# Four 128x32 matmuls in place of one 128x128 while attention runs, and w_in loaded in column quarters

## The chip, the cores and the metric

The kernel runs on one core of one Trainium2 chip. The metric is the device time of one execution in microseconds, as the median of several runs. Before the change it was 392.27 us (three runs, 391.82 to 393.17).

A core has one instruction stream for each engine: TensorE (PE, with its weight loads listed as PEld), VectorE (DVE), ScalarE (ACT), GpSimd (POOL) and SyncE (SP). [...] Loads here are issued by POOL, stores by SP and ACT.

## The reference

```python
scores = matmul(q, k.T) / sqrt(64)          # q, k, v: 8 batches x 12 heads x 448 tokens x 64
attn   = softmax(scores) @ v
x      = attn as 3584 tokens x 768
h      = x @ w_in                           # w_in: 768 x 2048
out    = (h * sigmoid(h)) @ w_out           # w_out: 2048 x 768, out: 3584 x 768 float32
```

The kernel takes and gives float32 in memory. Its loads convert to float16, and its sums are float32 in PSUM.

## The kernel before

**Attention.** Each batch has three groups of four heads. A unit is one batch, one group and a range of query tokens (batch 0 is cut in two pieces of 224 tokens, the other batches have one piece of 448). For a unit, `scores` (L376) multiplies K by Q with 32-row matmuls, four of them side by side because each head uses 32 rows of the array. `expo` (L412) takes the exponential on ACT. `attend` (L438) multiplies the exponentials by V, and `attend_sums` (L453) sums them; both use 128x32 matmuls, four side by side, one for each head and so for each 32 columns of the array. VectorE turns K and Q (L359, L369), inverts the sums and scales the result into x (L545).

**MoE.** `ffn1` (L557) multiplies x by w_in: six 128x128 matmuls for each 128 columns of w_in. ACT and VectorE make the activation (L573, L598) into the tile G. The second product takes G with w_out: `plain` (L780) for the first 256 tokens and `product` (L768) for the rest, where seven products of half the depth stand for eight (a Strassen step on the 2x2 blocks). For batches 4 to 7 the first product uses the same step, `pair_product` (L688), after attention has ended.

**Array shapes.** PE therefore changes between three kinds of shape: rows (32x128), columns (128x32) and full (128x128). The planner charges `SWITCH` for each change.

**What sets the order.** A planner inside the kernel (`Order`) runs the program once on paper, with a duration for each operation, and puts the instructions out in the order it finds. `load` estimates when a DMA lands from `DMA_ROW`, `DMA_RATE`, `DMA_START` and `DMA_TAIL`. The main loop prefers scores when `PACE` allows them, then a step of an MoE product that has begun (`in_steps`, `next_step`), then `attend` and new MoE products. Until the first `ffn1` step, PE fills its idle time with matmuls on a tile of zeros (`run_zeros`, L1614; the first 47 of them in one go).

**Loads.** POOL issues loads in a fixed order (L297 K, L303 Q, L324 V, L333 w_in, L341 w_out) into one queue. The order is K and Q of batch 0's first piece, its V, two more Q, w_in's first column half in three DMAs, a Q, K and Q of batch 1, w_in's second half in three DMAs, and then w_out and the rest. K, Q and V go through small rings of buffers. PE, DVE and ACT wait for the landings where they read the data.

Of the kernel before, what the change touches and what calls it, by code (L numbers as in the profile page):

```python
# [16 lines left out]
SWITCH = 0.094  # L17
PE_OUT = 0.20
HOP = 0.10
DMA_ROW = 0.022  # L20
DMA_RATE = 13570.0
DMA_START = 1.2
DMA_TAIL = 1.0


def mm(n):
# [65 lines left out]
class Order:  # L92


    def __init__(self, shy):
        self.now, self.shy = 0.0, shy
        self.free = {"PE": 1.0, "ACT": 2.1, "DVE": 1.2, "POOL": 1.2}
        self.wait = {"ACT": [], "DVE": []}
        self.pool = []
        self.dma_free = 0.0  # L100
        self.out = []
        self.mode = None
        self.steps = []
        self.busy = {e: 0.0 for e in self.free}
# [19 lines left out]
        op.busy += gap  # L124
        self.start(op)

    def in_steps(self, op, each, steps):

        assert not self.steps
        self.steps = [  # L130
            Op("PE", each, fn, tail=op.tail) for fn in steps
        ]
        self.steps[-1].then = lambda at: self.whole(op, at)
        self.next_step()
# [4 lines left out]
            op.then(at)  # L139

    def next_step(self):
        self.on_pe(self.steps.pop(0), "full")

    def load(self, rows, row_bytes, emit, ring=None, gate=None):
        op = Op("POOL", 0.58, emit)
# [3 lines left out]
    def step(self):  # L149

        soon = []
        for eng in ("ACT", "DVE"):
            if self.free[eng] > self.now:
                soon.append(self.free[eng])
                continue
            best, urgent = None, None
            for op in self.wait[eng]:
                at = op.ready()
                if at is None:
                    continue  # L160
                if at > self.now:
                    soon.append(at)
                    if op.bias <= -10 and (urgent is None or at < urgent):
                        urgent = at
                elif best is None or at + op.bias < best[0]:
                    best = (at + op.bias, op)
            if best and best[1].bias >= 0 and eng == "DVE" and urgent is not None:
                if urgent < self.now + self.shy * best[1].busy:
                    continue
            if best:  # L170
                self.wait[eng].remove(best[1])
                self.start(best[1])
                soon.append(self.free[eng])
        if self.free["POOL"] > self.now:
            soon.append(self.free["POOL"])
        elif self.pool:
            op, took, ring, gate = self.pool[0]
            at = 0.0
            if ring is not None:
                at = ring.when(1)  # L180
            if at is not None and gate is not None:
                g = gate()
                at = None if g is None else max(at, g)
            if at is not None and at <= self.now:
                self.pool.pop(0)
                if ring is not None:
                    ring.take()
                self.start(op)
                self.dma_free = max(self.dma_free, self.now + DMA_START) + took
                op.done = self.dma_free + DMA_TAIL  # L190
                soon.append(self.free["POOL"])
            elif at is not None:
                soon.append(at)
        return soon
# [3 lines left out]
def kernel(  # L198
# [9 lines left out]
    nc = tc.nc  # L208
# [5 lines left out]
    NG = NH // HG  # L214
# [19 lines left out]
    PAIRS = (B - 4, B - 2)  # L234
    LAST = {B - 4: range(DFF // 256), B - 2: range(DFF // 256)}
    NEAR = 0.15
    LATE = -2.0
    COLD, FIRST = 8.5, 47
    TURN = 8
    WHOLE = 10  # L240
# [5 lines left out]
    READ_B = -4  # L246
    PAIR_B = -2
    SILU_B = 0
    HOLD = 0.4
    SHY = 0.65  # L250
    TWB = 4
    SXB = 4
# [300 lines left out]

    h_t = {}

    def ffn1(b, f, t0, t1, cc):
        nc.tensor.matmul(  # L557
            out=h_t[(b, f, t0)][:, 0 : t1 - t0],
            lhsT=w_in_t[:, cc, 128 * f : 128 * (f + 1)],
            rhs=xc(b, cc)[:, t0:t1],  # L560
            start=(cc == 0),
            stop=(cc == NDC - 1),
            skip_group_check=True,
        )

    def gates_of(b, fs, t0, t1):
        r, n = b % 2, len(fs) * (t1 - t0)
# [194 lines left out]

    BANK = {1: 1, 2: 1, 6: 6, 7: 7, 4: 7, 5: 5, 3: 5}

    def product(qd, m, f):
        w = {1: rows(2 * qd, 0), 2: rows(2 * qd, 1), 4: rows(2 * qd + 1, 1), 7: rows(2 * qd + 1, 0)}
        w = w[m] if m in w else S_t[(qd, m)]
        nc.tensor.matmul(  # L768
            out=pr_t[(qd, BANK[m])][:, 0:OH],
            lhsT=w[:, f, :],  # L770
            rhs=W_[m][:, f, :],
            start=(f == 0 and BANK[m] == m),
            stop=(f == HF - 1),
            skip_group_check=True,
        )


    def plain(t, j, f0, f1):
        for f in range(f0, f1):
            nc.tensor.matmul(  # L780
                out=pr_t[("o", t, j)][:, 0:OH],
                lhsT=rows(t, f // HF)[:, f % HF, :],
                rhs=B_[f // HF, j][:, f % HF, :],
                start=(f == 0),
                stop=(f == NFF - 1),
                skip_group_check=True,
            )

    def take_plain(t, j):
        nc.scalar.copy(out=ost(t // 2, t % 2, j), in_=pr_t[("o", t, j)][:, 0:OH])  # L790
# [105 lines left out]
        plan_q(hg)  # L896
    plan_v(0, 0, NG)
    plan_q(NG)
    plan_q(NG + 1)
    plan_w_in(0, DFF // 2)  # L900
    plan_q(NG + 2)
    plan_k(1, 0)
    plan_q(NB0)
    plan_w_in(DFF // 2, DFF)
    plan_k(1, 1)
    plan_q(NB0 + 1)
    plan_w_out(0, NFF // 4)
    plan_w_out(NFF // 4, NFF // 2)
    plan_k(1, 2)
    plan_q(NB0 + 2)  # L910
    for hg in range(NG):
        plan_v(1, hg, hg + 1)
    plan_w_out(NFF // 2, 3 * NFF // 4)
    plan_w_out(3 * NFF // 4, NFF)
    for n in range(NB0 + NG, NU):
        b, hg = units[n][:2]
        plan_k(b, hg)
        plan_q(n)
        plan_v(b, hg, hg + 1)
# [35 lines left out]
    def queue_ffn1(b, g0, g1):  # L955
# [6 lines left out]
        for fs in turns:  # L962

            def run(fs=fs):
                n = t1 - t0
                op = Op("PE", len(fs) * NDC * mm(n), None, tail=PE_OUT)
                warm["on"] = False
                bank = m_ring.take()[0]
                for i, f in enumerate(fs):
                    h_t[(b, f, t0)] = P[:, bank, n * i :]  # L970
                od.in_steps(
                    op,
                    mm(n),
                    [
                        lambda f=f, cc=cc: ffn1(b, f, t0, t1, cc)
                        for f in fs
                        for cc in range(NDC)
                    ],
                )
                th = od.add(  # L980
                    Op(
                        "ACT",
                        act(n * len(fs)),
                        lambda: tanh(b, fs, t0, t1),
                        [op],
                        -3 if b == 0 else TANH_B,
                        tail=0.2,
                    )
                )
                g = Op(  # L990
                    "DVE",
                    n * len(fs) / 960.0 + 0.145,
                    lambda: gate(b, fs, t0, t1),
                    [th],
                    GATE_B,
                    then=m_ring.giver(bank),
                )
                od.add(g)
                for f in fs:
                    g_op.setdefault((b, f), []).append(g)  # L1000
                ffn1_left[b] -= 1
                ffn1_op[b].append(op)
# [203 lines left out]
    def queue_plain(t, j):  # L1206
# [8 lines left out]
        def queue(f0, f1):  # L1215
            def run():
                op = Op("PE", (f1 - f0) * mm(OH), lambda: plain(t, j, f0, f1), tail=PE_OUT)
                if f0 == 0:
                    bank.extend(m_ring.take())
                    pr_t[("o", t, j)] = P[:, bank[0]]  # L1220
                    ost_ring.take()
                od.on_pe(op, "full")
                parts.append(op)
                if f1 < NFF:
                    return
                plain_op[(t, j)] = op
                od.add(Op("ACT", act(OH), lambda: take_plain(t, j), [op], -2, then=then))
                if len(plain_op) == 4:
                    sums_w((1,))
# [54 lines left out]
    def queue_quad(qd):  # L1284
# [16 lines left out]
        def queue(m):  # L1301
            def run():
# [5 lines left out]
                    ring.take(need)  # L1308
                if m in (5, 6, 3):
                    op.then = sg_ring.give  # L1310
                od.in_steps(op, mm(OH), [lambda f=f: product(qd, m, f) for f in range(HF)])
                pr_op[(qd, m)] = op
                if m == 1:
                    read(1, "ACT", take_1, [op])
# [89 lines left out]
    for ns in jobs:  # L1404
# [6 lines left out]
            qk_seq.append((ns, 3, (0, 1)))  # L1411
        av_seq += [(ns, part) for part in range(3)]
    pace = {"next": 0.0}
    av_data = {"at": None}

    def qk_at():
# [192 lines left out]

    warm = {"on": 1, "first": 1}  # L1610

    def run_zeros(n):
        for _ in range(n):
            nc.tensor.matmul(  # L1614
                out=P[:, 7, 384:512],
                lhsT=zeros,
                rhs=zeros,
                start=True,
                stop=True,
                skip_group_check=True,  # L1620
            )

    while True:
        plan_turns(qk_seq[0][0][0] + 3 if qk_seq else NU)
# [46 lines left out]
        if warm["on"] and od.free["PE"] <= od.now and wait > 0.06 and od.now > 0.9:  # L1671
            each = mm(128) if od.now > COLD else 0.107
            n = max(1, int((wait - 0.06) / each), int(wait / each + 0.9) * (od.now < COLD))
            if warm.pop("first", None):
                n = FIRST
            od.on_pe(Op("PE", n * each, lambda n=n: run_zeros(n)), "full")
        od.now = min(later)
        assert od.now < 2000.0
    assert not (qk_seq or av_seq or moe or any(od.wait.values()) or od.pool)
# [32 lines left out]
```

## Time and profile before

| what | value |
|---|---|
| median of three runs | 392.27 us |
| profiled execution's span | 388.9 us |
| run time less span | 3.4 us |
| PE busy | 380.1 us (98%) |
| DVE, ACT, POOL busy | 295.0, 239.1, 83.6 us |
| PE instructions (matmuls, weight loads) | 3714 and 3714 |
| granted PE clock | 1.00 in every stretch read |
| DMA, software queue | 24784 packets, 22.82 MB |
| DMA, instruction queue q8 | 29 packets, 0.48 MB |

The profile lists one execution. A busy share is the time an engine had at least one instruction in progress. The chain of waits follows the work that ended last back to its start. In the list of groups, the count after x is the number of instructions, and the name after `<-` is what released the engine; "issue" means that the engine waited for nothing that the profile shows.

### The profile page before, as it was taken

To read this page: it belongs to the slowest core of one execution; us is meant where nothing else is said; L and a number is where in the kernel's file an instruction comes from. 1 tells how busy PE (TensorE), PEld (TensorE's weight loads), DVE (VectorE), ACT (ScalarE), POOL (GpSimd) and SP (SyncE) were. 2 spreads that over 40 slices of the span, in tenths; PEclk is the share of its full clock that TensorE was granted. 3 is DMA by queue.
4 is the path that set the end of the run, shared out by engine and by line. 5 is a ranking of instruction groups with operands and counts; after the bars stand their busy time and mean duration, and the time that the engine had idled before them with its cause. 6 is when DMAs were issued, how large, how long until landed. Compare 5 with 4: busy or idle time off the path is not lost.

```text
span 388.9 us, 9194 instructions
## 1 busy us (share of the span) xinstructions
PE 380.1 (98%) x3714; PEld 197.8 (51%) x3714; DVE 295.0 (76%) x531; ACT 239.1 (61%) x307; POOL 83.6 (22%) x153
## 2 busy tenths in 40 slices
PE   8989999999999999999999999999999999999996
PEld 7657775443444443444443444545556655556663
DVE  2455676898978877888887888999888747777662
ACT  4948885587977568876668885518781028872000
POOL 7632453601506060606060500000000000000000
PEclk9999999999999999999999999999999999999999
DMA  7999999751828574826775700320002330001333
GB/s 116 205 210 210 168 172 180 119 99 27 118 46 123 123 113 73 115 35 93 149 118 88 97 0 22 83 63 0 1 2 56 89 96 7 0 0 42 103 93 91
DMA packets 35579, 34.43 MB, mean 89 GB/s; under 512 B 11600, under 2 KB 34000, under 8 KB 35536
## 3 DMA queue, kind: packets, MB, share of 16 engines
q0 software_dynamic: 24784, 22.82, 39.4%
q1 hardware_dynamic: 9984, 10.24, 9.7%
q10 hardware_dynamic: 768, 0.79, 0.8%
q8 instruction: 29, 0.48, 0.5%
q14 instruction: 14, 0.11, 0.1%
HBM read 45.61 MB, written 11.01 MB: 146 GB/s over the span
## 4 chain that ended last, share of the span: by engine, by line
PE 95%; DMA 1%; DVE 1%; ACT 1%; issue 1%; ACTq 0%; POOLq 0%
PE P L768 31%; PE P L557 20%; PE P L688 16%; PE P L376 11%; PE P L438 10%; PE P L780 3%; PE P L1614 2%; PE P L453 2%; DMA rk<-in_k_dram 1%; ACT E L412 1%; DMA out_dram<-ost 0%; DVE xT L545 0%; DVE ost L820 0%; DVE R L494 0%; DVE KT L359 0%
## 5 line engine op out<-in xcount | busy, mean ns | idle before, releaser
L412 ACT ACTIVATE E<-P 128x1792 f16<-128x1792 f32 (+3 forms) x98 | 143.2, 1481 | 60.9 <-PE P L376 59.9
L557 PE MATMUL P<-xT,w_in_t 128*128 128x448 f16 (+1 forms) x480 | 81.0, 316 | 0.0
L324 POOL DMA_DIRECT2D V<-in_v_dram x84 | 45.9, 557 | 89.5 <-PE P L438 75.9
L557 PEld LDWEIGHTS <-w_in_t 128*128 128x128 f16 x480 | 43.4, 98 | 35.7 <-issue 14.9
L768 PEld LDWEIGHTS <-G 128*128 128x128 f16 x400 | 37.4, 98 | 31.0 <-issue 7.8
L376 PE MATMUL P<-rq,KT 32*128 32x448 f16 (+4 forms) x864 | 50.3, 340 | 0.9 <-ACT E L412 0.5
L598 DVE SCALAR_TENSOR_TENSOR G<-G,P 128x448 f16<-128x448 f16 x64 | 37.7, 611 | 10.3 <-ACT G L573 10.1
L768 PEld LDWEIGHTS <-S 128*128 128x128 f16 x312 | 29.8, 98 | 22.9 <-issue 3.8
L768 PE MATMUL P<-w_out_t,S 128*128 128x384 f16 x208 | 39.1, 326 | 0.0
L768 PE MATMUL P<-D,G 128*128 128x384 f16 x208 | 39.0, 326 | 0.0
L545 DVE SCALAR_TENSOR_TENSOR xT<-P,R 128x448 f16<-128x448 f32 (+1 forms) x54 | 29.0, 568 | 11.9 <-PE P L438 9.1
L820 DVE TENSOR_TENSOR ost<-P,u 128x384 f32<-128x384 f32 x39 | 21.6, 555 | 19.4 <-PE P L768 12.8
L768 PE MATMUL P<-w_out_t,G 128*128 128x384 f16 x192 | 35.9, 327 | 0.0
L438 PE MATMUL P<-E,V 128*32 128x448 f16 (+2 forms) x672 | 34.4, 356 | 0.0
L573 ACT ACTIVATE G<-P 128x448 f16<-128x448 f32 x64 | 32.8, 542 | 1.9 <-PE P L557 1.5
L688 PE MATMUL P<-sx,tw 128*128 128x448 f16 x144 | 30.0, 352 | 0.0
L376 PEld LDWEIGHTS <-KT 32*128 32x128 f16 (+2 forms) x864 | 14.3, 98 | 26.4 <-issue 23.6
L688 PEld LDWEIGHTS <-tw 128*128 128x128 f16 x192 | 18.8, 98 | 17.5
L423 DVE TENSOR_TENSOR T<-E,E 128x1792 f16<-128x1792 f16 x20 | 21.7, 1083 | 5.0 <-ACT E L412 5.0
L423 DVE TENSOR_TENSOR T<-T,E 128x1792 f16<-128x1792 f16 x20 | 21.7, 1085 | 4.9 <-ACT E L412 4.9
L438 PEld LDWEIGHTS <-V 128*32 128x32 f16 (+2 forms) x672 | 13.9, 95 | 20.0 <-issue 13.2
L824 ACT COPY u<-P 128x384 f32<-128x384 f32 x13 | 6.2, 477 | 27.7 <-PE P L768 27.3
(74 smaller groups left out, 442.2 us busy)
## 6 DMA issues: line engine op xcount, KB each, us to landing
out_dram<-ost SPq DMA_DIRECT2D x208, 48.0 KB, 1.7
rk<-in_k_dram POOLq DMA_DIRECT2D x24, 224.0 KB, 5.7
rq<-in_q_dram POOLq DMA_DIRECT2D x21, 224.0 KB, 5.7
w_in_t<-in_moe_w_in_dram POOLq DMA_DIRECT2D x6, 512.0 KB, 12.1
w_out_t<-in_moe_w_out_dram POOLq DMA_DIRECT2D x4, 768.0 KB, 13.1
V<-in_v_dram POOLq DMA_DIRECT2D x43, 64.0 KB, 3.7
V<-in_v_dram POOLq DMA_DIRECT2D x40, 48.0 KB, 3.9
out_dram<-ost ACTq DMA_DIRECT2D x16, 48.0 KB, 1.8
```

The costliest lines, as they stand in the source:

```text
L324: nc.gpsimd.dma_start(out=VT[(b, hg0)][32 * x : 32 * (x + 1), :, 0:count, :], in_=v[b, hs].rearrange("h (i g) d -> i h g d", g=TPP)[:, :, ...
L376: nc.tensor.matmul(out=pS[p0 : p0 + 32 * (x1 - x0), h % 2, at : at + nq], lhsT=KT[(b, hg)][32 * h : 32 * (h + 1), c, x0:x1, :, e], rhs=QT[ ...
L412: nc.scalar.activation(out=E[(n, w)][0:kr, 2 * y[0] : 2 * y[-1] + 2, 0:nk], in_=P[0:kr, bank : bank + 2 * len(y), 0:nk], func=AF.Exp, scal ...
L423: nc.vector.tensor_tensor(out=T[n], in0=T[n] if step else E[(n, 0)], in1=E[(n, step + 1)], op=ALU.add,)
L438: nc.tensor.matmul(out=a[32 * h : 32 * (h + 1), 0:nq], lhsT=w, rhs=e[k0:k1, h, at : at + nq], start=start, stop=stop, skip_group_check=True,)
L545: nc.vector.scalar_tensor_tensor(out=xc(b, cc)[:, 32 * g0 : 32 * g1], in0=acc[(n, part)][:, 0:nq], scalar=0.5, in1=rdn_t[n].rearrange("p g ...
L557: nc.tensor.matmul(out=h_t[(b, f, t0)][:, 0 : t1 - t0], lhsT=w_in_t[:, cc, 128 * f : 128 * (f + 1)], rhs=xc(b, cc)[:, t0:t1], start=(cc == 0),
L573: nc.scalar.activation(out=g, in_=h, func=AF.Tanh)
L598: nc.vector.scalar_tensor_tensor(out=g, in0=g, scalar=1.0, in1=h, op0=ALU.add, op1=ALU.mult)
L688: nc.tensor.matmul(out=pp_t[(*key, PBANK[m])], lhsT=w[:, c, :], rhs=xc(pb + x[0], 3 * x[1] + c) if isinstance(x, tuple) else sx_t[(pb, x)] ...
L768: nc.tensor.matmul(out=pr_t[(qd, BANK[m])][:, 0:OH], lhsT=w[:, f, :], rhs=W_[m][:, f, :], start=(f == 0 and BANK[m] == m), stop=(f == HF - 1),
L820: nc.vector.tensor_tensor(out=out, in0=a, in1=b, op=op)
```

## The change

1. `ffn1`, `product` and `plain` can issue each 128x128 matmul as four 128x32 matmuls. Strip j takes columns 32j to 32j+32 of the weights, the same moving operand, and writes PSUM partitions 32j to 32j+32. `strips(tiled)` gives the four strips, or one strip of 128. They are used as long as attention work is left (`moe_mode()` gives "cols"), and always in `plain`. `run_zeros` follows the shape in force.
2. w_in is loaded in column quarters (12 DMAs of 256 KB in place of 6 of 512 KB). The first quarter stands ahead of one Q of batch 0, and three quarters stand ahead of batch 1's first K and Q, with the fourth behind them. V of batch 1 is loaded earlier, each group after its K and Q or near it.
3. The planner's numbers for loads and for waiting change. No instruction's content depends on them, only the order.

```diff
-DMA_ROW = 0.022
-DMA_RATE = 13570.0
+DMA_ROW = 0.004
+DMA_RATE = 13350.0
 DMA_START = 1.2
-DMA_TAIL = 1.0
+DMA_TAIL = 1.4
+DMA_EARLY = 1.3
...
-        self.on_pe(self.steps.pop(0), "full")
+        self.on_pe(self.steps.pop(0), self.step_mode)
...
+                self.loads += 1
+                if self.loads == 2:
+                    self.dma_free += DMA_EARLY
...
-    LATE = -2.0
+    LATE = -0.3
...
-    HOLD = 0.4
+    HOLD = 0.0
...
+    def strips(tiled):
+
+        return [slice(32 * j, 32 * (j + 1)) for j in range(4)] if tiled else [slice(0, 128)]
+
+    def ffn1(b, f, t0, t1, cc, tiled):
+        w = w_in_t[:, cc, 128 * f : 128 * (f + 1)]
+        for at in strips(tiled):
+            nc.tensor.matmul(
+                out=h_t[(b, f, t0)][at, 0 : t1 - t0],
+                lhsT=w[:, at],
+                rhs=xc(b, cc)[:, t0:t1],
...
+        for at in strips(tiled):
+            nc.tensor.matmul(
+                out=pr_t[(qd, BANK[m])][at, 0:OH],
+                lhsT=w[:, f, at],
+                rhs=W_[m][:, f, :],
...
+            for at in strips(True):
+                nc.tensor.matmul(
+                    out=pr_t[("o", t, j)][at, 0:OH],
+                    lhsT=rows(t, f // HF)[:, f % HF, at],
...
     plan_q(NG)
+    plan_w_in(0, DFF // 4)
     plan_q(NG + 1)
-    plan_w_in(0, DFF // 2)
     plan_q(NG + 2)
+    plan_w_in(DFF // 4, DFF // 2)
+    plan_w_in(DFF // 2, 3 * DFF // 4)
     plan_k(1, 0)
     plan_q(NB0)
-    plan_w_in(DFF // 2, DFF)
+    plan_w_in(3 * DFF // 4, DFF)
+    plan_v(1, 0, 1)
     plan_k(1, 1)
     plan_q(NB0 + 1)
+    plan_v(1, 1, 2)
     plan_w_out(0, NFF // 4)
     plan_w_out(NFF // 4, NFF // 2)
     plan_k(1, 2)
     plan_q(NB0 + 2)
-    for hg in range(NG):
-        plan_v(1, hg, hg + 1)
     plan_w_out(NFF // 2, 3 * NFF // 4)
     plan_w_out(3 * NFF // 4, NFF)
+    plan_v(1, 2, 3)
...
+    def moe_mode():
+
+        return "cols" if qk_seq or av_seq else "full"
```

More of the change, by code (lines that the diff above doesn't have):

```diff
@@ L99, in __init__ @@
         self.pool = []
-        self.dma_free = 0.0
+        self.dma_free, self.loads = 0.0, 0
         self.out = []
@@ L125, in on_pe, with in_steps @@
         self.start(op)
-    def in_steps(self, op, each, steps):
+    def in_steps(self, op, each, steps, mode="full"):
         assert not self.steps
+        self.step_mode = mode
         self.steps = [
@@ L554 @@
     h_t = {}
[L556 to L564, printed above, removed]
+    def strips(tiled):
[7 more added lines that the diff above has]
+                rhs=xc(b, cc)[:, t0:t1],
+                start=(cc == 0),
+                stop=(cc == NDC - 1),
+                skip_group_check=True,
+            )
     def gates_of(b, fs, t0, t1):
@@ L763, with product @@
     BANK = {1: 1, 2: 1, 6: 6, 7: 7, 4: 7, 5: 5, 3: 5}
-    def product(qd, m, f):
+    def product(qd, m, f, tiled):
         w = {1: rows(2 * qd, 0), 2: rows(2 * qd, 1), 4: rows(2 * qd + 1, 1), 7: rows(2 * qd + 1, 0)}
         w = w[m] if m in w else S_t[(qd, m)]
[L768 to L775, printed above, removed]
+        for at in strips(tiled):
[3 more added lines that the diff above has]
+                rhs=W_[m][:, f, :],
+                start=(f == 0 and BANK[m] == m),
+                stop=(f == HF - 1),
+                skip_group_check=True,
+            )
     def plain(t, j, f0, f1):
         for f in range(f0, f1):
[L780 to L787, printed above, removed]
+            for at in strips(True):
+                nc.tensor.matmul(
+                    out=pr_t[("o", t, j)][at, 0:OH],
+                    lhsT=rows(t, f // HF)[:, f % HF, at],
+                    rhs=B_[f // HF, j][:, f % HF, :],
+                    start=(f == 0),
+                    stop=(f == NFF - 1),
+                    skip_group_check=True,
+                )
     def take_plain(t, j):
@@ L966, in run @@
                 op = Op("PE", len(fs) * NDC * mm(n), None, tail=PE_OUT)
+                tiled = moe_mode() == "cols"
                 warm["on"] = False
@@ L974, in run @@
                     [
-                        lambda f=f, cc=cc: ffn1(b, f, t0, t1, cc)
+                        lambda f=f, cc=cc: ffn1(b, f, t0, t1, cc, tiled)
                         for f in fs
@@ L978, in run @@
                     ],
+                    moe_mode(),
                 )
@@ L1221, in run @@
                     ost_ring.take()
-                od.on_pe(op, "full")
+                od.on_pe(op, "cols")
                 parts.append(op)
@@ L1310, in run @@
                     op.then = sg_ring.give
-                od.in_steps(op, mm(OH), [lambda f=f: product(qd, m, f) for f in range(HF)])
+                tiled = moe_mode() == "cols"
+                od.in_steps(
+                    op,
+                    mm(OH),
+                    [lambda f=f: product(qd, m, f, tiled) for f in range(HF)],
+                    moe_mode(),
+                )
                 pr_op[(qd, m)] = op
@@ L1610, with run_zeros @@
     warm = {"on": 1, "first": 1}
-    def run_zeros(n):
+    def run_zeros(n, tiled):
         for _ in range(n):
[L1614 to L1621, printed above, removed]
+            for at in strips(tiled):
+                nc.tensor.matmul(
+                    out=P[at, 7, 384:512],
+                    lhsT=zeros[:, at],
+                    rhs=zeros,
+                    start=True,
+                    stop=True,
+                    skip_group_check=True,
+                )
     while True:
@@ L1675 @@
                 n = FIRST
-            od.on_pe(Op("PE", n * each, lambda n=n: run_zeros(n)), "full")
+            tiled = od.mode == "cols"
+            op = Op("PE", n * each, lambda n=n, tiled=tiled: run_zeros(n, tiled))
+            od.on_pe(op, "cols" if tiled else "full")
         od.now = min(later)
```

## The prediction

> **What bounds the kernel.** I read the page first. PE is busy 98% of the span, and the chain of waits is 95% PE, so PE's own stream sets the end. What matters is PE time per piece of work, and the places where the stream itself stops.
>
> ```profile
> PE 380.1 (98%) x3714; PEld 197.8 (51%) x3714; DVE 295.0 (76%) x531; ACT 239.1 (61%) x307; POOL 83.6 (22%) x153
> DMA  7999999751828574826775700320002330001333
> q8 instruction: 29, 0.48, 0.5%
> ```
>
> The slices of DMA show a load burst up to about 60 us, with the engines full, and then a thinner stream. Next the chain of waits around 105 us (start, length, what), where PE changes shape without idle time:
>
> ```profile
> 52.56 0.87 PE P L438 x16
> ...
> 99.84 2.19 PE P L557 x11
> ...
> 105.41 2.22 PE P L768 x13
> 107.63 0.51 PE P L376 x8
> 108.14 0.68 PE P L453 x12
> 108.82 1.41 PE P L768 x8
> ```
>
> The two stretches of L768 differ by five matmuls and 0.81 us, so a full matmul of 384 columns takes 0.163 us, and 0.10 to 0.11 us of each stretch is left over. Eleven full ones of 448 columns give (2.19-0.11)/11=0.189. Row and column matmuls run four at a time: with 0.189 a group, 0.51-2x0.189=0.13, 0.68-3x0.189=0.11 and 0.87-4x0.189=0.11 are left over again. That rest is the price of a change of shape, and four column matmuls cost what one full one costs.
>
> Then the timelines of weight loads and matmuls where PE stops with no releaser, near 25 us:
>
> ```profile
> 24.74 0.12 PEld L438 LDWEIGHTS <-G 128*32 128x32 f16 x8
> 25.92 0.19 PEld L438 LDWEIGHTS <-G 96*32 96x32 f16 x8 [1.07 <-issue]
> 24.74 0.37 PE L438 MATMUL P<-E,G 128*32 128x224 f16 x7
> 25.92 0.45 PE L438 MATMUL P<-E,G 128*32 128x224 f16 x9 [0.81 <-issue]
> ```
>
> Sixteen equal matmuls stand in a row. The eighth, whose weights are already loaded, starts 1.07 us late, with no wait of its own, and the weight load behind it starts with it. I read this as a stream that had run out of instructions. The DMA view between 23.6 and 24.7 us, and one narrowed to 23.68 to 23.72, show an instruction packet that starts at 23.70:
>
> ```profile
> q8 instruction: 1, 0.02, 5.3%
> q8 instruction: 1, 0.02, 146.1%
> ```
>
> The last figure is a share of 16 engines' 0.04 us: the packet took 0.94 us, so it ended at 24.64, and PE went on 1.28 us after that. Table by stretch (us, then each engine's busy time and count, clock, DMA share, GB/s), cut where PE has issued 256 more instructions, counted from the stalled one:
>
> ```profile
> 14.38:20.27 5.89, 4.90 (x138) 3.27 (x131) 3.42 (x9) 5.25 (x7) 2.88 (x5) 1.00 1.13 212
> 20.27:24.86 4.59, 4.47 (x129) 3.20 (x129) 2.60 (x8) 3.60 (x5) 1.84 (x3) 1.00 1.14 208
> 24.86:33.37 8.51, 6.73 (x137) 4.86 (x130) 4.21 (x12) 3.87 (x5) 2.42 (x5) 1.00 1.13 211
> 33.37:41.62 8.25, 8.25 (x130) 6.38 (x131) 5.24 (x13) 6.92 (x9) 2.19 (x4) 1.00 1.15 210
> ```
>
> 29 packets for 7428 instructions is one per 256. The quickest 256 in the burst (4.59 us) end in the stall. So the stream is brought in blocks of 256 through the same DMA engines as the loads, and in the burst a block may come later than PE uses one up.
>
> **The change, part by part.** The sum is made against the profiled execution's own 388.9 us; the median is 3.4 us above it and I carry that along.
>
> Shape changes. Counting in the two orders every change of shape ahead of real work (zeros left out): 228 before, 201 after. 27 x 0.115 = 3.1 us gained. Streaming time is equal. Real work on PE by the pitches above (0.189, 0.163, 0.096 for 224 columns, 0.115 a change): 365.5 us before, 362.4 after. Before, the first `ffn1` stretch starts at 31.05 with 13.2 us of that work done; 17.8 us were lost by then, and from then to 60 us the loss stays 17.8. The rest (5.6 us) lies in later short waits and the tail.
>
> Instructions. Matmuls rise from 3714 to 6403, weight loads the same; 12806 in place of 7428, all of the rise while attention runs. In the after order 1280 instructions from the 962nd on (five blocks) hold 17.4 us of work, 3.5 us a block. Before, blocks there took 4.6 to 12 us.
>
> What a block costs in the burst: wait of the fetch + 0.94 + 1.28. Fetches start 3.3, 3.4, 2.1, 1.6 and 2.7 us after PE crosses a boundary (14.38 to 17.68, 20.27 to 23.70, 33.37 to 35.47, 41.62 to 43.26, 52.52 to 55.25), and 3.7 after the stall's end (25.92 to 29.62), the only case where PE stood at the boundary, as it will after the change. At 102.07, with thin DMA, the wait is 0.6; one at 73.03 even precedes its crossing (74.49), so requests leave about 1 us ahead of it and the 1.6 to 3.4 are low by that. Ends: 1.6+2.2=3.8 and 4.8+2.2=7.0 (the 4.8 is 24.86 to 29.62). I take 5.7, nearest the one starved case (5.9).
>
> Behind a PE that stands there, all of its queue waits: scores, so ACT's exponentials, so DVE's sums. If one fetch runs at a time, PE gets one block per 5.7 us. The second boundary (450th) is crossed near 14.2, when V has landed (last V issue about 6.4, 7.8 to landing) and the first `attend` on V can run. Seven blocks later, 14.2 + 7x5.7 = 54.1, PE stands at instruction 2242, with 26.0 us of work behind it by the after order. Before had done 54.1-17.8=36.3. That is 10.3 behind, less the 3.1: 7.2 slower. From there the burst ends, and a block's work (4.1 rising to 6.4 us) covers the fetch (0.6 to 2.7, + 2.2): 0, at most +2 where K, Q and V of a batch come together.
>
> [...]
>
> [...]
>
> Loads. Quarters: six more issues on POOL of 0.55 to 0.70 us, 3.9 at most; hidden, as POOL idles between issues (22% busy) and the queue is full. First quarter: Q before it landed by 14.55 at 0.21 MB per us, so 0.79 MB more is there at 18.3, ahead of its use (x of the first piece not before 23.2). Batch 1's first K and Q wait for more w_in: 0.79+0.11 MB or 4 us later than before (25.8), still ahead of 33. SP's stores keep their places.
>
> Order. In the after order the first `attend` on V stands ahead of the scores of unit 2, which before ran at 10.88 and 12.42 while V was on its way (`attend` at 15.07); they now wait for V at 14.2. ACT, fed by scores alone, has the exponentials of units 0 and 1 until about 15 (eight of 0.92 from 7.9 on): at most 0.3. 11 more zeros at 0.107 precede the first scores: 1.2 us later; ACT is 94% busy from 10 to 20 us, so this can show, 0 to 1.2, but lies beneath the fetch stalls. Without those, starting `ffn1` earlier could win back up to 4.4 us of idle between 15 and 30; I take 0 for both together.
>
> **The rivals.**
> (a) The fetch keeps up: several blocks are held, or two fetches run at once. For: just one such stall in the whole trace. Against: its place. Then only the 3.1 remains: 389.2 us, with the early idle won back as low as 386. This is the other side; it decides where a block takes under 4.7 us in the burst (14.2+7x4.7=47.1, when before had done 29.3: 3.3 behind, what the shapes gain).
> (b) The fetch limits, but shorter: at 5.0 us a block (2.8 mean wait from crossing + 2.2) the boundary comes at 49.2, 31.4-26.0=5.4 behind, 2.3 slower: 394.6.
> (c) It limits at 7.0: six blocks by 56.2, 22.5 of work against 38.4, 12.8 slower: 405.
> (d) The change of shapes saves nothing, since the row matmuls of the scores still lie between MoE products: 392.3. The orders say 27 fewer, so only the price could fail.
>
> **How the numbers follow.** Forecast 392.3 + 7.2 = 399.5. Chances: fetch-bound with 5.2 to 6.5 us a block 0.45; (b) and below, down to no change, 0.15; (c) 0.10; (a) 0.25; (d) 0.05. The likeliest one's own range is 396 to 404. The range needs part of (a): 388.5 to 405. A difference of 0.3% (1.2 us) is about what runs of this kernel can tell. Slower by more than that: 0.45+0.10+ most of (b), 0.68; same: 0.06; faster: 0.26.
>
> **What would show it.** Right: PE rows with "issue" as releaser, 1 to 3 us each, between 18 and 58 us; about 50 instruction packets, one each 5 to 6 us in the burst; PE's tenths below 9 in slices 2 to 6; the long run of pair products starting some 7 us later than before's 258.3 us. Wrong: PE full from 31 us on and instruction packets 3 to 4 us apart in the burst. Wrong in size only: stalls, but in sum under 5 us or over 15. If stalls go on beyond 60 us, the thin stage was priced too low.

## The result, and the profile after

The change makes the kernel slower: 403.82 us in the median of four executions (402.56 to 404.08), against 392.19 us before on the same chip (four executions, 391.82 to 393.17). The ratio is 1.0268, with a 95% interval of 1.0213 to 1.0322 (the two medians alone give 1.030). The forecast was 399.5 us in a range of 388.5 to 405.0. The profiled execution has a span of 401.9 us, 13.0 more than the one of before. The medians differ by 11.6. The profiled execution of before was a quick one: where both are known, the time is 1.8 us above the span, so its 388.9 us stand for about 390.7. One execution of a later experiment (438.79 us at a mean granted clock of 0.842, the loads and numbers alone) was in a slow state and is left out, with its profile.

From the page of the kernel after, the same lines as were shown of before, with PE's own rows of the slices:

```profile
span 401.9 us, 14600 instructions
PE 381.8 (95%) x6403; PEld 207.5 (52%) x6403; DVE 295.2 (73%) x531; ACT 239.4 (60%) x307; POOL 88.0 (22%) x159
PE   8787778999999999999999999999999999999996
PEclk9799899999999999999999999999999999999999
DMA  8999997238183859292939250130001231001433
q8 instruction: 50, 0.82, 0.8%
```

PE is busy for almost the same time as before (381.8 us against 380.1), though it issues 2689 more matmuls. What is added is idle time, and all of it that the slices show lies in the first seven slices (10 us each), in which DMA stays at 7 to 9 tenths. There are 50 instruction packets in place of 29.

The waits of PE (line waited at, what ended the wait, us in total, times, longest):

```profile
PE P L568 <- issue: 5.0, 4, 2.1
PE P L443 <- issue: 3.7, 2, 3.0
PE P L443 <- DMA G<-in_v_dram: 2.8, 1, 2.8
PE P L381 <- issue: 1.0, 2, 0.6
```

Waits without a releaser now add up to 9.7 us at the first MoE product (L568), at `attend` (L443) and at the scores (L381). The third line is another kind: one wait of 2.8 us for a V that had not landed. Here are single steps of the chain of waits that carry these (start, length, what):

```profile
26.13 1.24 issue
...
41.88 2.97 issue
...
54.57 2.13 issue
```

To see that these waits are the fetch, the span is cut where PE has issued 256 more instructions, as was done for the kernel before. The first boundary below is the 962nd instruction by the prediction's count, which runs about eight ahead of the trace (954 of PE's instructions start before 27.36 us). The columns are (us, busy time and count of PE, PEld, DVE, ACT, POOL, then clock, DMA share, GB/s):

```profile
27.37:33.30 5.93, 4.22 (x131) 2.81 (x132) 2.89 (x8) 3.76 (x5) 2.35 (x5) 1.00 1.24 202
33.30:38.12 4.82, 3.73 (x131) 2.93 (x131) 2.03 (x7) 3.76 (x5) 4.27 (x8) 1.00 1.18 167
38.12:44.86 6.74, 3.77 (x129) 3.02 (x130) 3.17 (x8) 2.75 (x3) 3.62 (x6) 1.00 1.11 195
44.86:50.79 5.93, 5.43 (x132) 4.20 (x132) 2.18 (x5) 2.01 (x2) 1.09 (x2) 0.71 1.15 210
50.79:56.71 5.92, 3.79 (x131) 2.99 (x132) 1.86 (x3) 3.27 (x5) 1.10 (x2) 1.00 1.20 205
56.71:61.81 5.10, 4.41 (x132) 2.85 (x132) 1.24 (x2) 3.71 (x4) 2.73 (x5) 1.00 1.06 158
61.81:67.26 5.45, 5.01 (x130) 3.15 (x131) 4.47 (x8) 3.34 (x4) 1.01 (x2) 1.00 0.54 90
67.26:70.99 3.73, 3.73 (x127) 2.77 (x131) 2.85 (x6) 2.54 (x3) 1.72 (x4) 1.00 0.85 92
```

Seven blocks take 39.9 us, 5.7 each, while PE is busy for 3.7 to 5.4 us in each. The next block takes 3.73 us and PE is busy all through it. Two narrow windows of the DMA view (0.04 us each, 48.51 to 48.55 and 54.43 to 54.47) hold the start of one instruction packet each:

```profile
q8 instruction: 1, 0.02, 146.2%
q8 instruction: 1, 0.02, 152.2%
```

The packets take 0.94 and 0.97 us (the share times 16 engines times 0.04 us). They start at 48.52 and 54.45, so they end at 49.46 and 55.42, and PE crosses its next boundary at 50.79 and 56.71, which is 1.3 us after each end. Over eight boundaries running, 33.30 to 70.99, PE crossed 1.28 to 1.52 us after the end of the packet; at the first seven of them it had stood idle before. The time from a crossing to the start of the next packet was 2.5 to 4.3 us up to 65 us, and 1.3 us behind the crossing at 67.26.

To say where the 13 us arise I take the time that has passed less the real work that PE has done, by the pitches of the prediction (0.189, 0.163 and 0.096 us for a group of 448, 384 and 224 columns, 0.115 us a change of shape):

| time lost up to | 27.4 us | 40 us | 56.7 us | 67.3 us | 255 us | 380 us |
|---|---|---|---|---|---|---|
| before | 16.9 | 18.0 | 18.0 | 18.0 | 18.8 | 19.2 |
| after | 19.0 | 22.6 | 30.8 | 32.7 | 35.0 | 35.5 |
| difference | 2.1 | 4.6 | 12.8 | 14.7 | 16.2 | 16.3 |

16.3 us more are lost and 3.1 us less work is to be done, 13.2 us in sum, against 13.0 in the spans.

### The profile page after: what moved, and what is told of

The parts are those of the page before. It is cut to its first block, busy times and chain, and to the rows that moved or that the text cites. A ratio compares the mean times of both kernels' runs of the same rounds, so it can differ in the third digit from the quotient of the medians.

```text
span 401.9 us, 14600 instructions
## 1 busy us (share of the span) xinstructions
PE 381.8 (95%) x6403; PEld 207.5 (52%) x6403; DVE 295.2 (73%) x531; ACT 239.4 (60%) x307; POOL 88.0 (22%) x159
## 4 chain that ended last, share of the span: by engine, by line
PE 90%; issue 3%; DMA 2%; POOL 1%; DVE 1%; ACT 1%; SPq 0%; DVEq 0%; ACTq 0%; POOLq 0%
PE P L780 30%; PE P L568 20%; PE P L699 16%; PE P L443 10%; PE P L381 10%; PE P L793 3%; DMA G<-in_v_dram 2%; PE P L458 2%; DVE xT L550 0%; PE P L1644 0%; POOL G L329 0%; POOL rk L302 0%; DMA out_dram<-ost 0%; POOL rq L308 0%; DVE ost L833 0%
## 5 line engine op out<-in xcount | busy, mean ns | idle before, releaser
L568 PE MATMUL P<-xT,w_in_t 128*32 128x448 f16 (+1 forms) x1920 | 84.3, 321 | 5.0 <-issue 5.0
L568 PEld LDWEIGHTS <-w_in_t 128*32 128x32 f16 x1920 | 48.2, 98 | 38.3 <-issue 18.4
L780 PEld LDWEIGHTS <-G 128*32 128x32 f16 (+1 forms) x976 | 39.4, 97 | 29.2 <-issue 6.2
L381 PE MATMUL P<-rq,KT 32*128 32x448 f16 (+4 forms) x864 | 51.8, 344 | 1.5 <-issue 1.0
L609 DVE SCALAR_TENSOR_TENSOR G<-G,P 128x448 f16<-128x448 f16 x64 | 37.8, 612 | 14.7 <-ACT G L584 14.0
L780 PEld LDWEIGHTS <-S 128*32 128x32 f16 (+1 forms) x744 | 30.9, 97 | 21.6 <-issue 3.8
L584 ACT ACTIVATE G<-P 128x448 f16<-128x448 f32 x64 | 33.1, 542 | 11.6 <-PE P L568 11.3
L550 DVE SCALAR_TENSOR_TENSOR xT<-P,R 128x448 f16<-128x448 f32 (+1 forms) x54 | 29.0, 568 | 14.7 <-PE P L443 11.0
L780 PE MATMUL P<-D,G 128*32 128x384 f16 (+1 forms) x496 | 39.5, 327 | 0.0
L780 PE MATMUL P<-w_out_t,S 128*32 128x384 f16 (+1 forms) x496 | 38.6, 326 | 0.0
L833 DVE TENSOR_TENSOR ost<-P,u 128x384 f32<-128x384 f32 x39 | 21.6, 553 | 19.0 <-PE P L780 13.7
L443 PE MATMUL P<-E,V 128*32 128x448 f16 (+2 forms) x672 | 34.6, 355 | 0.4 <-DVE xT L550 0.4
L780 PE MATMUL P<-w_out_t,G 128*32 128x384 f16 (+1 forms) x480 | 35.0, 327 | 0.0
L381 PEld LDWEIGHTS <-KT 32*128 32x128 f16 (+2 forms) x864 | 14.8, 100 | 27.4 <-issue 25.4
L699 PEld LDWEIGHTS <-tw 128*128 128x128 f16 x192 | 18.8, 98 | 17.5
L443 PEld LDWEIGHTS <-V 128*32 128x32 f16 (+2 forms) x672 | 15.0, 95 | 18.7 <-issue 10.5
L308 POOL DMA_DIRECT2D rq<-in_q_dram x27 | 15.1, 559 | 40.2 <-PE P L381 27.4
```

What stands on the lines that cost most here:

```text
L381: nc.tensor.matmul(out=pS[p0 : p0 + 32 * (x1 - x0), h % 2, at : at + nq], lhsT=KT[(b, hg)][32 * h : 32 * (h + 1), c, x0:x1, :, e], rhs=QT[ ...
L443: nc.tensor.matmul(out=a[32 * h : 32 * (h + 1), 0:nq], lhsT=w, rhs=e[k0:k1, h, at : at + nq], start=start, stop=stop, skip_group_check=True,)
L550: nc.vector.scalar_tensor_tensor(out=xc(b, cc)[:, 32 * g0 : 32 * g1], in0=acc[(n, part)][:, 0:nq], scalar=0.5, in1=rdn_t[n].rearrange("p g ...
L568: nc.tensor.matmul(out=h_t[(b, f, t0)][at, 0 : t1 - t0], lhsT=w[:, at], rhs=xc(b, cc)[:, t0:t1], start=(cc == 0), stop=(cc == NDC - 1), sk ...
L584: nc.scalar.activation(out=g, in_=h, func=AF.Tanh)
L609: nc.vector.scalar_tensor_tensor(out=g, in0=g, scalar=1.0, in1=h, op0=ALU.add, op1=ALU.mult)
```

## The experiments

The theory: the strips make more instructions of the same work (a block of 256 holds 3.5 us of it, where blocks of before took 4.6 to 12 us), and in the load burst PE then waits for each block of 256 instructions, because the packets that bring them queue behind the loads. Rivals: the new order of loads and the new planner numbers are what costs (V late); or the strips are slow in themselves; or the loads have nothing to do with it, and the fetch is too slow at any time. The wait for V and a drop of PE's granted clock behind it, told of further below, are a rival too.

### The loads and numbers alone

The strips are taken away, and the new loads and planner numbers stay:

```diff
     def moe_mode():
-        return "cols" if qk_seq or av_seq else "full"
+        return "cols" if False else "full"
...
-            for at in strips(True):
+            for at in strips(tiled):
...
-            tiled = od.mode == "cols"
+            tiled = False
```

> The change without its strips: loads in the new order, the planner's new numbers, every MoE matmul whole. 3681 matmuls, 226 changes of shape. Three theories. F (fetch): PE's instructions come in blocks of 256, one per about 5.8 us while the load burst lasts, and four strips use a block up in 3.5 us. F expects 390 to 393 here, no PE idle time put down to issue in sum over 1.5 us, lost time by 70 us near 18 to 19.5 (the late V may show by 1 to 2). L (loads and order are the loss): 399 or more. S (a strip costs more than its share of the whole matmul): 390 to 393, as F.

Measured: 393.76 us, ratio 1.0006 (0.9969 to 1.0044): no difference that can be told, though the median lies just above the 390 to 393 that was expected. This kernel has 3681 matmuls in place of 3714, as the planner's numbers also set how many matmuls on zeros are put in. Each execution has a mean granted clock on record, and the nine used here fall in two groups. Four with a clock of 0.996 to 1.00 took 390.06 to 391.47 us. Five with a clock of 0.982 to 0.987 took 393.59 to 395.57 us. Of 25 executions of the kernel before on that chip only one had less than 0.99. So the loads and numbers alone save about 1 us where the clock holds, and an execution takes some 3 to 4 us more where it drops.

### The strips alone

The strips stay, and the loads, their order and the planner's numbers are those of before:

```diff
-DMA_ROW = 0.004
-DMA_RATE = 13350.0
+DMA_ROW = 0.022
+DMA_RATE = 13570.0
-DMA_TAIL = 1.4
-DMA_EARLY = 1.3
+DMA_TAIL = 1.0
+DMA_EARLY = 0.0
...
-    LATE = -0.3
+    LATE = -2.0
...
-    plan_w_in(0, DFF // 4)
     plan_q(NG + 1)
+    plan_w_in(0, DFF // 2)
...
```

> The strips alone, on the loads and the planner's numbers of before: 6487 matmuls, 199 changes of shape, w_in in halves. F expects 399 to 405: at work of 26 us PE stands at instruction 2372, a few more than in the change, so the burst costs the same or a little more, and the late V costs less. L expects 389 (3 us fewer than before). S expects 400 to 403, with the loss spread over the whole of attention, not before 70 us.

Measured: 404.89 us, ratio 1.0299 (1.0251 to 1.0347). The strips alone carry the whole loss (12.6 us against 11.6). The waits of PE in this kernel:

```profile
PE P L568 <- issue: 7.3, 4, 2.6
PE P L443 <- issue: 3.1, 2, 2.1
...
PE P L1641 <- issue: 1.8, 2, 1.2
PE P L381 <- issue: 1.5, 1, 1.5
```

There is no wait for V among them, and 13.7 us with "issue". The mean granted clock of this execution was 0.996, with 0.50 only from 26.3 to 29.7 us. So the loss comes without the wait for V and with little of the drop in the clock. The fetch waited 3.5 to 3.8 us after a crossing six times running, and a block took 5.9 us. Its w_in comes in rows of 2 KB, as in the kernel before (whose page counts 1536 packets of 2 KB to under 8 KB), in place of the change's 1 KB (whose page counts none), from about 14 to 32 us, and the waits that begin in that time are 3.53, 3.64 and 3.84 us (3.7 in the mean). In the changed kernel w_in's rows of 1 KB land from 13 to 33 us, and the waits there are 3.08, 2.97 and 3.63 us (3.2 in the mean). That is 0.5 us less, but an effect of the row length is not shown: under w_out's rows of 1.5 KB the changed kernel waited 3.7 to 4.3 us, and this one 3.6 to 4.3.

### Strips only after the burst

Strips are used only once the planner's clock is past 62 us. First with the loads and numbers of the change:

```diff
     def moe_mode():
-        return "cols" if qk_seq or av_seq else "full"
+        return "cols" if (qk_seq or av_seq) and od.now > 62.0 else "full"
```

and `plain` follows `moe_mode()` too, with the zeros in full shape.

> The change, but strips only from 62 us of the planner's time on, when the burst is nearly over. 5625 matmuls, 208 changes of shape. F expects 2.1 us (18 changes at 0.115) less than the untiled kernel of this job, so 388 to 391, with issue idle under 2 us. L expects the same time as the untiled one or the change, about 400. S expects more than the untiled one, by up to 10 us, since most strips are still there.

Then the same on the loads and numbers of before:

> Loads and the planner's numbers of before, strips only from 62 us of the planner's time on. F expects before less about 2 us: 389.5 to 391. L expects the same, 389 to 390. S expects 395 or more.

Measured: 390.5 us, ratio 0.9948 (0.9912 to 0.9984), with the new loads, and 391.53 us, ratio 0.9962 (0.9934 to 0.9990), with the old ones, half a microsecond above the range expected. Both still issue many more matmuls than before (5625 and 5706, against 3714). From the page of the first, and from the waits of PE:

```profile
PE   7789999999999999999999999999999999999996
q8 instruction: 44, 0.72, 0.8%
```

```profile
PE P L443 <- DMA G<-in_v_dram: 2.1, 1, 2.1
```

PE is full from the fourth slice on, with 44 instruction packets, and no wait of PE is listed with "issue" in the kernel with the new loads. So strips outside the burst cost nothing, and what they save shows. The time lost stays at 17 us from 40 to 70 us, where the changed kernel lost 10 more. What remains is the wait for V, which the kernel with the old loads doesn't have.

### Two strips of 64

```diff
     def strips(tiled):
-        return [slice(32 * j, 32 * (j + 1)) for j in range(4)] if tiled else [slice(0, 128)]
+        return [slice(64 * j, 64 * (j + 1)) for j in range(2)] if tiled else [slice(0, 128)]
```

> The change with two strips of 64 columns in place of four of 32, so half of the extra instructions; the shape now differs from that of attention on V, so every change of shape is back (about 228). F expects a block of 256 instructions to last 64 matmuls' time, 6.2 us and more even at 224 columns, over the 5.8 of a fetch: few stalls, 391 to 395. L expects about 402 plus the shape changes, 405. S expects about half of the loss: 397 to 400.

Measured: 394.31 us, ratio 1.0049 (1.0019 to 1.0078). It has 4591 matmuls, and all the changes of shape are back. Its page and its waits of PE:

```profile
PE   8789999999999999999999999999999999999996
q8 instruction: 36, 0.59, 0.6%
```

```profile
PE P L443 <- DMA G<-in_v_dram: 1.6, 1, 1.6
...
PE P L443 <- issue: 0.9, 2, 0.7
PE P L381 <- issue: 0.9, 1, 0.9
```

With a third of the extra instructions, the waits with "issue" fall from 9.7 to 1.8 us, and the time lost at 55 us from 29.1 to 18.6. Half the strips save nothing on changes of shape, so there is only a small loss and no gain. So the loss goes with the number of instructions, and not in proportion: here, where a block holds more work than in the change, a third of the extra instructions brings little of the waits.

### All strips, but without the loads of the weights

w_in and w_out are filled by POOL with a constant in place of the loads:

```diff
-        nc.gpsimd.dma_start(
-            out=w_in_t[:, 2 * c : 2 * c + 2, f0:f1],
...
+        nc.gpsimd.memset(w_in_t[:, 2 * c : 2 * c + 2, f0:f1], 0.01)
...
-        nc.gpsimd.dma_start(
-            out=w_out_t[:, f0:f1],
...
+        nc.gpsimd.memset(w_out_t[:, f0:f1], 0.01)
```

> The change with w_in and w_out filled by POOL with a constant instead of loaded: the products are then not the reference's, and 6.3 MB of loads are left out of the first 60 us. All instructions of PE stay. F expects the fetches to start within 1 us of PE's crossing a block boundary once K, Q and V of batch 0 are in, so hardly a stall behind 20 us and 388 to 393 in all. L, if it is the order of instructions that costs, expects 398 or more. S expects 400 to 403.

Measured: 390.75 us, ratio 0.9948 (0.9919 to 0.9977), with all 6403 matmuls. Its waits of PE, and the table by stretch for three blocks that begin with the 1218th instruction:

```profile
PE P L435 <- DMA G<-in_v_dram: 3.0, 1, 3.0
...
PE P L435 <- issue: 1.0, 1, 1.0
...
PE P L560 <- issue: 0.4, 1, 0.4
```

```profile
30.97:34.43 3.46, 3.46 (x139) 2.92 (x131) 1.66 (x5) 3.07 (x5) 3.46 (x2) 1.00 0.38 49
34.43:37.98 3.55, 3.55 (x140) 2.98 (x129) 3.27 (x9) 1.78 (x3) 3.55 (x4) 1.00 0.60 86
37.98:41.49 3.51, 3.51 (x132) 2.94 (x135) 2.95 (x9) 2.89 (x3) 3.51 (x3) 1.00 0.30 55
```

The same kind of blocks takes 3.5 us in place of 5.7, and PE is busy all the time. Packets start 0.9 to 1.1 us after the crossings at 30.97, 34.43 and 37.98. The next two blocks, up to 51.09 us, took 4.2 and 5.4 us: K, Q and V were landing again (DMA share 0.80 and 1.18), the packets started 2.0 and 3.1 us after the crossings, and PE stood for 0.4 and 1.0 us. The same stream of instructions is thus as quick as the sum said once the DMA engines have room. This rules out strips that are slow in themselves, and a fetch that is too slow at any time. The wait for V (3.0 us) is still there, and so is the drop of the clock behind it (0.50 from 14.2 to 21.0 us), so these two alone do not make the loss. By the table's measure this kernel loses 23.9 us up to 380 us, the change 35.5 and before 19.2: of the 16.3 us, 11.6 go with the loads of the weights. Leaving them out also takes away any wait for w_in itself, of which the change lists none. It is not a kernel that could be had, as its products are not those of the weights.

### The wait for V

`LATE` is the planner's allowance that decides when `attend` may be placed; a lower value puts it later. First on the whole change:

```diff
-    LATE = -0.3
+    LATE = -1.3
```

> The change with LATE -1.3 in place of -0.3, so that the planner counts on V a microsecond later and puts the first half of unit 2's scores ahead of the first attend on V. Strips and loads as in the change. In the change PE stood 2.77 us at that attend and the granted clock then was 0.5 from 14.4 to 21.2 us. F with the late V as a separate loss: the wait shrinks by about 1 us and the drop of the clock may go, 400.5 to 403; the stalls at block boundaries stay. If the late V were the main loss (L): under 396.

Measured: 402.57 us, ratio 1.0242 (1.0198 to 1.0286): 1.25 us less than the change, with intervals that overlap. The waits of PE:

```profile
PE P L568 <- issue: 7.6, 4, 2.6
PE P L381 <- issue: 2.9, 2, 2.4
PE P L443 <- issue: 1.3, 1, 1.3
```

The third row is the wait at the first `attend` on V, which starts at 14.84 us here as in the change: 1.3 us in place of 2.8. It is listed with "issue", but it stands some twelve instructions ahead of the block boundary. The clock stayed at 1.00 up to 22.7 us. But PE then stood for 2.4 us at the next block boundary, up to 21.3 us, which the change had crossed too late to wait at. By 27.4 us the time lost is 18.2 us, against 19.0 in the change. While the fetch is the bound, much of what an earlier wait gives up is taken by the next one.

The same edit on the kernel with late strips and new loads:

> Strips from 62 us of the planner's time on, the change's loads, LATE -1.3. F expects the time of the kernel with late strips (390.5) less 0 to 1 us: 389.5 to 390.5. L and S have no reason for a difference to that kernel.

Measured: 387.7 us (387.35 to 389.94), ratio 0.9874 (0.9836 to 0.9912). That is 2.8 us less than the same kernel with `LATE` at -0.3. It is below the 389.5 to 390.5 that was expected, and faster than both kernels of this case. Its page and the waits of PE:

```profile
PE   8889999999999999999999999999999999999996
```

```profile
PE P L381 <- ACT E L417: 1.7, 4, 0.9
PE P L443 <- DMA G<-in_v_dram: 1.4, 1, 1.4
```

The wait for V is 1.4 us, and the granted clock was 0.996 or more in all six executions. With `LATE` at -0.3 it was below 0.99 in five of ten. Part of the 2.8 us thus goes with the clock and not with the wait, which is only 0.7 us shorter.

The last edit for V adds to this kernel a later place for the planner's `DMA_EARLY`:

```diff
-                if self.loads == 2:
+                if self.loads == 3:
```

> As e8_late_strips_later_attend, and DMA_EARLY added at the third load in place of the second, where the trace has the gap (Q of the first unit landed at 5.5 us, the planner had 6.8): 11 zeros fewer ahead of the first scores, which come 1.2 us earlier. ACT is nearly full there, so up to 1.2 us less than e8_late_strips_later_attend; the attend on V stays bound by V. Expected 388.5 to 390.5.

Measured: 387.95 us, ratio 0.9871 (0.9835 to 0.9907). This is no gain over the one before it, where up to 1.2 us was expected.

### Where the burst ends for the fetch

Strips from planner time 45 us on, in place of 62:

```diff
-        return "cols" if qk_seq or av_seq else "full"
+        return "cols" if (qk_seq or av_seq) and od.now > 45.0 else "full"
```

> The change's loads and numbers, strips from 45 us of the planner's time on, so that the last 15 to 20 us of the burst have them. F expects three or four blocks of 3.5 us of work at 5.8 us each, so 6 to 8 us more than with strips from 62 (390.5), and the stalls only between 45 and 65 us: 396 to 399. S expects the same as with strips from 62, plus under 1 us, as only 150 more matmuls are cut.

Measured: 396.14 us, ratio 1.0066 (1.0031 to 1.0101). From the waits and the chain of its profile:

```profile
PE P L568 <- issue: 2.3, 1, 2.3
PE P L443 <- issue: 2.0, 1, 2.0
```

```profile
58.01 2.29 issue
```

The wait of 2.0 us ends at 14.7 us, ahead of any strip of the MoE products: it is the wait for V, at the same instruction as in the kernel with strips from 62 us. Up to 56.7 us this kernel has lost 20.0 us, and 24.2 by 67.3: 4.2 us in a stretch that the prediction had given to the thin stage. The granted clock in that stretch was 0.85 and 0.83 in its two halves, so a part of the 4.2 is the clock. Its ten executions lay between 392.26 us at a mean clock of 0.998 and 397.78 us at 0.978. With strips from 62 us, the two executions at 0.999 took 387.51 and 388.43 us, so at much the same clock the strips from 45 us cost about 4 us more. Strips cost in this stretch too.

The two kernels also price a drop of the clock. They issue the same matmuls up to the 820th, at about 50 us, and both wait for V, 2.1 us with strips from 62 and 2.0 with strips from 45. In the first profile the clock stayed at 1.00. In the second it was 0.50 from 16.0 to 26.3 us, and the 821st matmul started at 53.38 in place of 50.17 us. That drop cost 3.2 us.

## Why the prediction was right, and where it was not

**The direction and its cause held.** In the burst PE is bound by the fetch of its instructions, and this is the largest part of the loss (11.6 of 16.3 us go with the weight loads). The strips alone lose what the change loses (404.89 us), late strips are not slower than before (ratio 0.9948), and neither is the full number of strips without the weight loads (ratio 0.9948 too). Rival (a), that the fetch keeps up, is refuted for the burst and right for the rest of the attention stage. In the burst no store of blocks ahead showed: PE crossed eight boundaries running 1.28 to 1.52 us after the end of the block's own packet and had stood idle before the first seven, and 5.7 us a block was not hidden behind blocks in which PE was busy for 3.7 to 5.4 us.

**The cost of a block was right.** 5.7 us was taken, from bounds of 3.8 and 7.0. The seven blocks from the 962nd instruction on took 5.7 each, the seven from the 450th to the 2242nd 5.8 each (15.99 to 56.71 us). The parts held too: 2.5 to 4.3 us until the packet starts, 0.94 us for the packet, 1.3 us until PE goes on. Rivals (b) with 5.0 and (c) with 7.0 are out; (c)'s time of 405 is close to the measured one for another reason, below.

**The start of the burst was early by 1.8 us.** The prediction had the 450th instruction at 14.2 us, as V lands; it was crossed at 15.99. Its block had landed at 13.2, so here it wasn't the fetch: PE stood for V. The first `attend` on V started at 14.84, 0.6 us later than V was put, and from there to the boundary PE ran for 1.15 us at a clock of 0.50, for which the prediction had no term. The order was priced too low as well: scores behind the first `attend` on V were put at "at most 0.3" us, argued from ACT alone. With late strips, a wait for V that was 0.7 us shorter (2.1 to 1.4) lowered the time lost by 27.4 us by the same 0.7 (16.2 to 15.5), at a clock of 1.00 in both. These are the two stalls in the timeline of PE (start, length, instruction, count, idle time before it and releaser):

```profile
14.84 0.94 PE L443 MATMUL P<-E,G 128*32 128x224 f16 x16 [2.77 <-DMA G<-in_v_dram]
...
44.86 0.74 PE L443 MATMUL P<-E,G 128*32 128x224 f16 x14 [2.97 <-issue]
45.21 3.50 PE L568 MATMUL P<-xT,w_in_t 128*32 128x224 f16 x68
```

At the end of both stalls the granted clock was halved. The trace records 0.50 from 14.38 to 21.21 and from 45.10 to 48.52 us, and 1.00 from 4 us on otherwise, up to 400 us. The table by stretch shows it (the first row starts with the `attend` at 14.84, the second, with a part at 1.00, with the one at 44.86):

```profile
14.84:21.20 6.36, 6.36 (x136) 4.59 (x140) 2.61 (x7) 2.55 (x4) 5.03 (x8) 0.50 1.24 204
44.86:48.70 3.84, 3.84 (x86) 3.25 (x90) 1.25 (x4) 0.54 (x1) 0.54 (x1) 0.56 1.16 213
```

The group of 68 strips of L568 took 3.50 us, where 17 groups by 0.096 are 1.63. This second drop was hidden: PE still stood for 0.5 us at the next boundary (50.79), which came 1.3 us after its packet. The prediction had no term for the clock, which was 1.00 in every stretch of before that was read. With the 0.1 us more per block, the 2242nd instruction was crossed at 56.71 in place of 54.1 us. By then PE had done 25.9 us of work (26.0 were forecast), and before had done 38.7. That is 12.8 us behind, in place of 10.3.

**The end of the burst was early.** "From there the burst ends" is the step that failed: after the 2242nd instruction PE still waited for two blocks, until 67.26 us, and lost another 1.9 us. The prediction read the burst of before as lasting to about 60 us and ended the count at 54.1; its own line of DMA shows nine tenths up to the seventh slice, which ends at 68 us. The loads of K, Q and V behind w_out go on there (a DMA share of 1.06 and 0.54 in the two blocks), and strips from 45 us on lose 4.2 us in just this stretch, the drop of the clock included.

**The thin stage** was priced at 0, at most 2, and lost 1.6 us. The changes of shape were priced at 3.1 us saved; strips after the burst bear most of this out. With the loads of before, late strips have 19 changes fewer (2.2 us by the price) and a ratio of 0.9962 (0.9934 to 0.9990), about 1.5 us, so rival (d), that they save nothing, is refuted. The kernel with a later `attend` and the new loads has a profiled span of 385.8 us, 3.1 below before, with 21 changes fewer (2.4 us less work by the pitches) and 0.6 us less lost.

So the sum goes 10.3 (forecast at the 2242nd) + 2.5 (late boundary) + 1.9 (two more blocks) + 1.6 (thin stage) - 3.1 = 13.2 us, against 13.0 in the spans and the forecast's 7.2. The loads were put at nothing, and without strips the time is that of before, within the interval of 0.9969 to 1.0044. The forecast of 399.5 was 4.3 us short of the median: the mechanism was right, while the times of its start and end were not. That the miss stayed in the range is in part luck. 403.8 us is at the edge of the likeliest case's own 396 to 404, and the room above it came from rival (c), whose 7.0 us a block did not come.

**What stays open.** For the change itself the wait for V and the drop of the clock behind it were not separated; a drop of 10.2 us cost 3.2 us with strips from 45 us, and the one here lasted 6.8. What makes the clock drop after some stalls and not after others was not settled: in the profiled kernel with strips after 62 us, V's wait was 2.1 us and the clock stayed at 1.00, and with strips from 45 us a wait of 2.0 us was followed by a drop.

## What to carry to other kernels

Count instructions as well as streaming time: where a split multiplies the instructions of an engine, cut its trace into blocks of what one packet brings (256 instructions here: 50 packets for 12806), and compare each block's work with the time that a fetch takes at that place, from the crossing to the packet, and on to the next crossing. In this kernel the split pays only in stages where the DMA engines have room: moving the same split behind the load burst turned 2.7% slower into 0.5% faster, and 1.3% faster with one wait shortened. Where such a bound sets the pace, work that is saved elsewhere in the same stage may show little: a wait 1.5 us shorter and a clock that held for longer brought 0.8 us by 27.4 us, as PE then stood for 2.4 us at the next block.

## What the runs showed of the hardware

- The granted clock of PE fell to 0.50 for 6.8 us at the end of a stall of 2.77 us, and for 3.4 us behind one of 2.97 us, in the middle of the kernel. The kernel before shows 1.00 in the same stretches. Drops in mid-kernel of other kernels lasted 3.4 us (the strips alone, 26.3 to 29.7 us), 6.8 us (without the weight loads, 14.2 to 21.0 us) and 10.2 us (strips from 45 us).
- With late strips and the new loads, ten executions lay between 387.51 us at a mean clock of 0.999 and 392.95 us at 0.981. So a spread of over 1% between executions of one kernel came with the clock. With a shorter wait for V, six executions had 0.996 or more.
- While the loads fill the DMA engines, an instruction packet starts late: 3.5 to 3.8 us after a crossing with the strips alone, 2.5 to 4.3 us in the change. In three blocks without the weight loads it was 0.9 to 1.1 us. The packet's own time in the change was 0.89 to 1.02 us up to 66 us, and 0.88 to 1.54 us behind that.
